# Two Newton steps, folded constants, a copy on Pool and wider w_down rows in a decode kernel

## The chip, the cores and the metric

The kernel runs on one core of a Trainium2 chip. The metric is device time in microseconds (us) of one execution, smaller is better. A core has five engines with queues of their own: PE (matrix products; its weight loads are listed as PEld), DVE and ACT (elementwise work and reductions), Pool (elementwise work, no access to the accumulators), and SP, which here only issues transfers. Work on one engine runs in program order; between engines only semaphores order it.

## The reference, cut to what matters

Two layers of a decoder for one new token of four sequences (B = 4, D = 512). In each layer an attention block with a cache of 4096 positions (32 query heads on 8 key/value heads of width 128) and a gated block (F = 1792):

```python
def _layernorm(x, eps=1e-5):
    m = jnp.mean(x, axis=-1, keepdims=True); v = jnp.var(x, axis=-1, keepdims=True)
    return (x - m) / jnp.sqrt(v + eps)

def _A_ref(x, k_cache, v_cache, wq, wo):          # attention with cached k, v
    q = (x @ wq).reshape(B, Sq, Hq, Dh)...
    p = _softmax(jnp.einsum("bhqd,bhkd->bhqk", q, k) * Dh ** -0.5)
    return einsum("bhqk,bhkd->bhqd", p, v)... @ wo

def _B_ref(x, w_gate, w_up, w_down):
    h = _sigmoid(x @ w_gate) * (x @ w_up)
    return h @ w_down

x = x + _A_ref(_layernorm(x), ...); x = x + _B_ref(_layernorm(x), ...)   # layer 1
x = x + _A_ref(_layernorm(x), ...); x = x + _B_ref(_layernorm(x), ...)   # layer 2, same weights and caches
```

## The kernel before

The caches are 64 blocks of 1 MB (K and V, for 4 sequences and 8 heads); together with the weights some 123 MB come in. Twelve slots of 1 MB hold blocks. Layer 2 reads the same caches, and part of them (K of heads 4 to 7, V of heads 6 and 7) is kept from layer 1 where the order allows; the rest is loaded again. `ORDER` writes out by hand in which order the 64 pairs of layer, sequence and head are worked on, two heads at a step; `loads` is the matching list of transfers, and `pump` issues the next ones on SP as soon as a slot is free. The eight parts of w_o and the parts of w_gate, w_up and w_down are spread between the first blocks of the caches (`wparts`).

One step of the main loop takes two heads through: `k_turn` (L872) transposes a K block in place on DVE in 32 x 32 squares; `q_blocks` (L646) lays the query out on Pool; `scores` (L889) multiplies on PE; `smax` (L904), `spread_max` (L909) and `softmax` (L919, L927) find the maximum and take exp; `ptrans` (L943, L975) turns the probabilities, with 16 small copies on ACT; `pv` (L991) multiplies with V of the step before, and `do_wo` (L1048, L1062) with w_o, adding into the residual `xT`.

When one sequence is through its attention in layer 1, its way to layer 2 is a *pass*: `pass_steps(b)` lists twelve parts, which PLACE2 and PLACE3 put into the gaps of the next two steps:

- `ln_a` (L479 to L504) sums x over partitions with a matmul by ones, centres it (`xc_sb`), copies that to bf16 (`xc_bf`, L499, on ACT) and squares it. `ln_b` (L556 to L544) sums the squares, and finds 1/sqrt(v + eps) by a first guess in integer arithmetic (L573) and three Newton steps: `newton_one` for one sequence, two instructions a step (L513, L521), `newton_many` for four, three a step (L533, L538, L544). The result `rs` isn't multiplied into x; it is applied to the products later. The Newton steps are written without their factors 1/2, so `rs` is off by a constant, which `RS` mends.
- `gate_row`, `up_row` (L707, L734): the products with w_gate and w_up as rows, x as weights of one column, four strips of the PE at once; tanh on ACT (L722) with the scale `rsg` (L717), and on DVE (t + 1) times up (L744). `h_turn` (L755) turns the row back to columns with four matmuls, `down` (L817) multiplies with w_down, and L827 and L837 scale and add to x.
- `ln_a`, `ln_b` again for the next layer, `q_row` twice (L772), `q_turn` (L800), `q_spread` (L620), which writes `qs` through ACT (L631).

The first norm and query, and the last norm and gated block, are done for all four sequences at once (`q_mm`, `gate_up` L660 with w_gate and w_up as weights, L1234 for w_down), the last after all attention. `_Sched` only records which instruction reads and writes which named buffer and puts semaphore waits before the instruction; the order on an engine is the order of the calls.

## Time and profile before

| | |
|---|---|
| time, median of 3 runs | 329.44 us (329.06 to 331.96) |
| the profiled execution | 330.95 us, its span 329.0 us |
| PE matmul busy | 229.4 us (70%) |
| DVE busy | 189.9 us (58%) |
| ACT busy | 144.8 us (44%) |
| Pool busy | 26.6 us (8%) |
| loaded | 122.95 MB, 374 GB/s over the span |

The span is the time from the first to the last instruction in the trace; the time of the execution has some 2 us around it. A row of the page's slices splits the span in 40 parts of 8.2 us and gives tenths of busy time, PEclk the clock granted to PE in tenths, GB/s what the transfers moved. In the timeline a row has start, duration, engine, line of the kernel, operation, what is written and read, how many, and in brackets how long the engine was idle before and what released it. In the view by windows a row has the stretch, its length, the busy time (and count) of PE, PEld, DVE, ACT and Pool, the granted clock, the share of the transfer engines and GB/s. The chain of waits is followed back from the last instruction, at each step to what released it.

### The profile page before, as it was taken

Reading aid. Unit: us, or ns where it says so; the run is one execution under the profiler, and the core shown is the slowest. Engines: PE = TensorE matmul, PEld = TensorE weight load, DVE = VectorE, ACT = ScalarE, POOL = GpSimd, SP = SyncE. Lnnn points to the kernel's source line nnn. Section 1 sums busy time; section 2 is a strip of 40 time slices with the busy share of each in tenths; the row PEclk is TensorE's granted clock in tenths of the full one; section 3 lists DMA queues with packets and bytes.
Section 4 is the critical chain, followed back from the end, with each engine's and each line's share of the span. In section 5 each row is a group of like instructions: output and inputs, shape, how many; then the busy total and the mean of one; then the engine's idle time right before and its main releaser. Section 6 shows DMA issues by size and latency. Waiting matters only on the chain.

```text
span 329.0 us, 10566 instructions
## 1 busy us (share of the span) xinstructions
PE 229.4 (70%) x4412; PEld 157.4 (48%) x4412; DVE 189.9 (58%) x446; ACT 144.8 (44%) x599; POOL 26.6 (8%) x133
## 2 busy tenths in 40 slices
PE   1335614232298986869899686889878688988976
PEld 1313412221255654645656464565456456555865
DVE  6377343432474439966644896664984666429543
ACT  2005412212045177644537664453765455267620
POOL 0001000000000011000001100000110000011000
PEclk9999999999997655555775555577555557555555
DMA  7999999999999999999999999999999999999600
GB/s 277 427 422 410 400 404 401 402 375 397 404 421 416 388 342 422 419 422 415 420 360 380 417 426 416 418 408 362 368 421 426 417 415 397 383 343 423 250 2 4
DMA packets 22838, 123.63 MB, mean 376 GB/s; under 512 B 2052, under 2 KB 7944, under 8 KB 8968
## 3 DMA queue, kind: packets, MB, share of 16 engines
q1 hardware_dynamic: 22792, 122.96, 93.2%
q8 instruction: 35, 0.57, 0.7%
q14 instruction: 11, 0.09, 0.1%
HBM read 122.95 MB, written 0.00 MB: 374 GB/s over the span
## 4 chain that ended last, share of the span: by engine, by line
PE 41%; DMA 32%; SPq 15%; DVE 7%; issue 3%; POOL 1%; ACT 1%; DVEq 0%; POOLq 0%; ACTq 0%
DMA slot<-in_A_v_cache_dram 28%; PE O_ps L991 12%; SPq L349 8%; PE S_ps L889 7%; SPq L363 6%; DVE slot L872 4%; PE M_ps L772 4%; DMA slot<-in_A_k_cache_dram 3%; PE MS L909 3%; PE O_ps L1048 2%; PE M_ps L817 2%; PE M_ps L707 2%; PE MS L950 2%; DVE small L904 1%; PE M_ps L479 1%
## 5 line engine op out<-in xcount | busy, mean ns | idle before, releaser
L872 DVE STREAM_TRANSPOSE slot<-slot 128x2048 f32<-128x2048 f32 (+1 forms) x62 | 112.5, 1814 | 41.1 <-DMA slot<-in_A_k_cache_dram 41.1
L975 ACT ACTIVATE pT<-PT 32x64 bf16<-32x64 f32 x504 | 108.4, 215 | 61.8 <-PE PT L943 50.1
L991 PE MATMUL O_ps<-pT,slot 128*128 128x4 bf16 x2048 | 62.3, 166 | 34.2 <-DMA slot<-in_A_v_cache_dram 32.6
L991 PEld LDWEIGHTS O_ps<-pT,slot 128*128 128x128 bf16 x2048 | 63.1, 105 | 40.2 <-DMA slot<-in_A_v_cache_dram 33.3
L889 PE MATMUL S_ps<-slot,qz 128*16 128x512 bf16 x512 | 60.3, 620 | 5.3 <-POOL qz L646 4.7
L646 POOL COPY qz<-qs 32x32 bf16<-32x32 bf16 x128 | 26.1, 204 | 277.1 <-PE S_ps L889 142.7
L927 ACT ACTIVATE pe<-S_ps,small 128x512 bf16<-128x512 f32 x32 | 22.0, 686 | 51.7 <-issue 45.9
L909 PE MATMUL MS<-valid_f,small 128*128 128x64 f32 x64 | 21.5, 438 | 32.6 <-DVE small L904 32.6
L909 PEld LDWEIGHTS MS<-valid_f,small 128*128 128x128 f32 x64 | 15.6, 304 | 50.2 <-DVE small L904 43.5
L904 DVE TENSOR_REDUCE small<-S_ps 128x1 f32<-128x512 f32 x32 | 21.3, 666 | 16.0 <-PE S_ps L889 16.0
L1048 PEld LDWEIGHTS O_ps<-oT,wo 128*128 128x128 bf16 x640 | 19.4, 105 | 12.7 <-issue 11.9
L889 PEld LDWEIGHTS S_ps<-slot,qz 128*16 128x16 bf16 x512 | 12.4, 109 | 25.0 <-issue 18.4
L1048 PE MATMUL O_ps<-oT,wo 128*128 128x2 bf16 (+1 forms) x640 | 20.3, 166 | 0.6 <-DVE oT L1029 0.6
L1029 DVE TENSOR_TENSOR oT<-O_ps,small 128x8 bf16<-128x8 f32 (+1 forms) x33 | 5.5, 167 | 20.9 <-PE O_ps L991 20.9
L950 PE MATMUL MS<-small 128*128 128x8 f32 x64 | 17.5, 347 | 0.0
L950 PEld LDWEIGHTS MS<-small 128*128 128x128 f32 x64 | 15.9, 306 | 0.0
L958 DVE RECIPROCAL small<-MS 128x8 f32<-128x8 f32 x32 | 6.6, 207 | 15.5 <-PE MS L950 15.1
L919 DVE CUSTOM_DVE_ANT_0 MS<-MS,small 128x64 f32<-128x64 f32 x32 | 8.8, 276 | 8.5 <-PE MS L909 8.5
L772 PE MATMUL M_ps<-wq,small 128*1 128x512 bf16 x128 | 13.2, 556 | 0.0
L631 ACT ACTIVATE qs<-M_ps 128x128 bf16<-128x128 f32 x8 | 1.9, 280 | 24.7 <-PE M_ps L620 24.7
L943 PE MATMUL PT<-ident_bf,pe 128*128 128x64 bf16 x128 | 11.8, 230 | 1.3 <-ACT pe L927 1.3
L479 PE MATMUL M_ps<-small 128*128 128x4 f32 (+1 forms) x20 | 5.9, 369 | 5.5 <-DVE small L837 2.1
(86 smaller groups left out, 147.3 us busy)
## 6 DMA issues: line engine op xcount, KB each, us to landing
slot<-in_A_v_cache_dram SPq DMA_DIRECT2D x56, 1024.0 KB, 12.8
slot<-in_A_k_cache_dram SPq DMA_DIRECT2D x48, 1024.0 KB, 12.0
wq<-in_A_wq_dram SPq DMA_DIRECT2D x4, 1024.0 KB, 7.9
wo<-in_A_wo_dram SPq DMA_DIRECT2D x8, 512.0 KB, 16.1
wg<-in_B_w_gate_dram SPq DMA_DIRECT2D x4, 448.0 KB, 13.7
wu<-in_B_w_up_dram SPq DMA_DIRECT2D x4, 448.0 KB, 14.3
wd<-in_B_w_down_dram SPq DMA_DIRECT2D x2, 896.0 KB, 16.5
out_dram<-slot SPq DMA_DIRECT2D x4, 1.0 KB
```

What stands on the lines that cost most here:

```text
L349: S.dma("sp", (lambda dst, src: lambda e: e.dma_start(dst, src))(dst, src), f"wo{n}" if kind == "wo" else kind, writes=[f"{kind}{n}"])
L646: (lambda a, ps: lambda e: e.tensor_copy(qz_sb[ps, :, :, a, :], qs_sb[b][ps, :, u * REP:(u + 2) * REP].rearrange("p t (u r) -> p u t r", r ...
L772: (lambda k, st: lambda e: e.matmul(M_ps[h][32 * st:32 * st + 1, :], lhsT=xc_bf[:, k, 0:1], rhs=wv[:, k, h, :, st, :], start=(k == 0), sto ...
L872: dve(lambda e: e.transpose(kf, kf), writes=[f"s{st}"])
L889: (lambda t, b2, e_, c, r0, ul: lambda e: e.matmul(S_ps[p][r0:r0 + 4 * REP, :], lhsT=qz_sb[:, ul, t, :, :].rearrange("p a r -> p (a r)"), ...
L904: dve(lambda e: e.tensor_reduce(rm_sb, S_ps[p][:, :], AX.X, ALU.max), reads=[f"S{p}"], writes=["rm"])
L909: lambda e: e.matmul(MS[:, 0:16 * REP], lhsT=rm_sb.broadcast_to([P, P]), rhs=valid_f[:, :], start=True, stop=True),
L927: lambda e: e.activation(pe_sb.rearrange("p j m -> p (j m)"), S_ps[p][:, :], ACTF.Exp, bias=nm_sb, scale=exp_scale, accum_out=sm_sb,),
L950: lambda e: e.matmul(MS[:, 64:64 + 2 * REP], lhsT=sm_sb.broadcast_to([P, P]), rhs=head_f, start=True, stop=True),
L975: (lambda dst, frm: lambda e: e.activation(dst, frm, ACTF.Copy))(dst, frm),
L991: (lambda x, c, j: lambda e: e.matmul(O_ps[p][:, ul * REP:(ul + 1) * REP], lhsT=vv[:, x * JG + c * 4 + j, :], rhs=pT_sb[:, x, j, 2 * ul + ...
L1048: (lambda c, r: lambda e: e.matmul(O_ps[p][:, 64 + 2 * c:64 + 2 * c + nb], lhsT=wo_sb[:, us[0] * REP + r, c * P:(c + 1) * P], rhs=oT_sb[:, ...
```

## The change

- Newton has two steps rather than three, with another first guess and other constants (`RSQRT_MAGIC`, `NEWTON_1`, `NEWTON_2`).
- The constant that mends `rs` (`RS`, and 0.5 RS ahead of the gated block) is multiplied into the bf16 copy of centred x (`mult`) rather than into later results. So `rsg` (L717) and the scaling of `eye4` (L1200) go, L827 and L837 become one instruction, and some instructions lose a factor.
- The bf16 copy of a single sequence (8 of them) is done on Pool; that of four sequences stays on ACT, with a scale. A key `pf` orders it against the query blocks on Pool.
- w_down is loaded with two neighbouring rows of the matrix side by side in a partition, 2 KB at a time, the first part 8 blocks of rows and the second 6 (before: 7 and 7, rows of 1 KB). For that the order of h changes: w_gate and w_up are read in blocks of 256 columns by the rows, and with every second column as weights in `gate_up`; `h_turn` takes every second column too.

The diff, without the dropped buffers and the renamed arguments of the calls:

```diff
-    RSQRT_MAGIC = float(0x5F375A86)
+    RSQRT_MAGIC = float(0x5F1FFFF9)
+    NEWTON_1 = 2.38924456
+    NEWTON_C = 0.703952253
+    NEWTON_2 = 3.0 / NEWTON_C ** 2
-    RS = -1.0 / 8192.0
+    RS = 0.5 * NEWTON_C ** 3 * (1.0 + 3.1e-7)
...
-        "wd": lambda n: (wd_sb[:, n * KH:(n + 1) * KH, :],
-                         B_w_down[n * KH * P:(n + 1) * KH * P, :].rearrange("(k p) n -> p k n", p=P)),
+        "wd": lambda n: (wd_sb[:, 8 * n:min(8 * n + 8, KF), :].rearrange("p (k e) n -> p k e n", e=2),
+                         B_w_down[8 * n * P:min(8 * n + 8, KF) * P, :].rearrange("(k p e) n -> p k e n", p=P, e=2)),
...
-    def ln_a(b0, nb):
+    def ln_a(b0, nb, mult):
...
-        act(
-            lambda e: e.activation(xc_bf[:, :, 0:nb], xc_sb[:, :, 0:nb], ACTF.Copy),
-            reads=["rc"],
-            writes=["xcb"],
-        )
+        if nb == 1:
+            S.inst(
+                "pool",
+                lambda e: e.tensor_scalar(xc_bf[:, :, 0:nb], xc_sb[:, :, 0:nb], mult, None, op0=ALU.mult),
+                reads=["rc"] + QZ,
+                writes=["xcb", "pf"],
+            )
+        else:
+            act(
+                lambda e: e.activation(xc_bf[:, :, 0:nb], xc_sb[:, :, 0:nb], ACTF.Copy, scale=mult),
...
-        for it, three in enumerate((3.0, 12.0, 768.0)):
+        for it, three in enumerate((NEWTON_1, NEWTON_2)):
...
-                reads=[f"qs{b}"],
+                reads=[f"qs{b}", "pf"],
...
-                        lhsT=wsb[:, k, fc * P:(fc + 1) * P],
+                        lhsT=wsb[:, k, bass.ds(fc // 2 * 2 * P + fc % 2, P, step=2)],
...
-        wv = wg_sb.rearrange("p k (f d) -> p k f d", d=P)
+        wv = wg_sb.rearrange("p k (f d) -> p k f d", d=2 * P)
...
-                nt = (KF - st + 3) // 4
+                nt = (KW - st + 3) // 4
...
-                        M_ps[0][32 * st:32 * st + 1, 0:nt * P],
+                        M_ps[0][32 * st:32 * st + 1, 0:nt * 2 * P],
...
-        dve(
-            lambda e: e.tensor_scalar(rsg[:, :], rs[:, 0:1], 0.5 * RS, None, op0=ALU.mult),
...
-            lambda e: e.activation(t_row[:, :], M_ps[0][:, :], ACTF.Tanh, scale=rsg[:, 0:1]),
+            lambda e: e.activation(t_row[:, :], M_ps[0][:, :], ACTF.Tanh, scale=rs[:, 0:1]),
...
-                    M_ps[0][:, 4 * j:4 * j + 4], lhsT=row_sb[:, 0, j * P:(j + 1) * P], rhs=strips, start=True, stop=True
+                        M_ps[0][:, bass.ds(8 * t + e_, 4, step=2)],
+                        lhsT=row_sb[:, 0, bass.ds(2 * P * t + e_, P, step=2)],
+                        rhs=strips,
...
-            lambda e: e.tensor_tensor(
-                dn_sb[:, :, 0:nb],
-                M_ps[0][:, 128:128 + KD * nb].rearrange("p (k b) -> p k b", k=KD),
-                bc(rs[:, 0:nb], KD, nb),
-                ALU.mult,
-            ),
...
-                out=xT[:, :, bsl(b0, nb)], in0=dn_sb[:, :, 0:nb], scalar=0.5 * RS, in1=xT[:, :, bsl(b0, nb)],
+                out=xT[:, :, b0], in0=M_ps[0][:, 128:128 + KD], scalar=rs[:, 0:1], in1=xT[:, :, b0],
                 op0=ALU.mult, op1=ALU.add,
...
-            lambda: ln_a(b0, 1),
+            lambda: ln_a(b0, 1, 0.5 * RS),
...
-    dve(lambda e: e.tensor_scalar(eye4, eye4, 0.5 * RS, None, op0=ALU.mult), writes=["eye4"])
```

More of the change, by code (lines that the diff above doesn't have):

```diff
@@ L225, in bass_interleave_layers__gqa_block_cached__glu_gated_glu__decode_kernel @@
     rowk_f = small(1)
-    rsg = small(1)
     rm_sb = small(1)
@@ L237, in bass_interleave_layers__gqa_block_cached__glu_gated_glu__decode_kernel @@
     nt_b = small(Bn)
-    nt_c = small(Bn)
     lnsum, lnsq = nt_a, nt_b
@@ L497, in ln_a @@
         )
-        act(
-            lambda e: e.activation(xc_bf[:, :, 0:nb], xc_sb[:, :, 0:nb], ACTF.Copy),
-            reads=["rc"],
-            writes=["xcb"],
-        )
+        if nb == 1:
[8 more added lines that the diff above has]
+                lambda e: e.activation(xc_bf[:, :, 0:nb], xc_sb[:, :, 0:nb], ACTF.Copy, scale=mult),
+                reads=["rc"],
+                writes=["xcb"],
+            )
         dve(
@@ L530, in newton_many @@
         y, yk = y0, "y0i"
-        for it, three in enumerate((3.0, 12.0, 768.0)):
+        for it, three in enumerate((NEWTON_1, NEWTON_2)):
             dve(
@@ L600, in q_mm @@
             dve(
[L601 to L607 removed]
+                lambda e: e.tensor_tensor(
+                    qT_sb[:, 0:HQ * nb].rearrange("p (h b) -> p h b", h=HQ),
+                    M_ps[0][:, 0:HQ * nb].rearrange("p (h b) -> p h b", h=HQ),
+                    bc(rs[:, 0:nb], HQ, nb),
+                    ALU.mult,
                 ),
@@ L752, in h_turn @@
         fns = []
-        for j in range(4):
-            fns.append(
-                (lambda j: lambda e: e.matmul(
-                    M_ps[0][:, 4 * j:4 * j + 4], lhsT=row_sb[:, 0, j * P:(j + 1) * P], rhs=strips, start=True, stop=True
-                ))(j)
-            )
+        for t in range(2):
+            for e_ in range(2):
+                fns.append(
+                    (lambda t, e_: lambda e: e.matmul(
+                        M_ps[0][:, bass.ds(8 * t + e_, 4, step=2)],
+                        lhsT=row_sb[:, 0, bass.ds(2 * P * t + e_, P, step=2)],
+                        rhs=strips,
+                        start=True,
+                        stop=True,
+                    ))(t, e_)
+                )
         S.group("pe", fns, reads=["ra"] + IDENT, writes=["M0"])
@@ L805, in q_turn @@
         dve(
-            lambda e: e.tensor_scalar(qT_sb[:, 0:HQ], M_ps[0][:, 0:HQ], RS, None, op0=ALU.mult),
+            lambda e: e.tensor_copy(qT_sb[:, 0:HQ], M_ps[0][:, 0:HQ]),
             reads=["M0"],
```

42 lines of the change are left out of this document (14 added, 28 removed).

## The prediction

> **What bounds the kernel now.** I read the page first: span, slices, chain of waits.
>
> ```profile
> span 329.0 us, 10566 instructions
> PEclk9999999999997655555775555577555557555555
> DMA  7999999999999999999999999999999999999600
> GB/s 277 427 422 410 400 404 401 402 375 397 404 421 416 388 342 422 419 422 415 420 360 380 417 426 416 418 408 362 368 421 426 417 415 397 383 343 423 250 2 4
> PE 41%; DMA 32%; SPq 15%; DVE 7%; issue 3%; POOL 1%; ACT 1%; DVEq 0%; POOLq 0%; ACTq 0%
> ```
>
> The transfer engines are busy in nearly every slice, so this is a streaming kernel, but the rate is not level: it dips in slices 14, 20 and 21, 27 and 28, 33 to 35 (slices of 8.2 us). Those are the four passes, in which one batch row's second half of a layer and the next query are squeezed between attention steps. The last three slices move almost nothing. The view by windows gives the level and the dips:
>
> ```profile
> 69.00:76.00 7.00, 4.39 (x86) 2.86 (x86) 2.45 (x3) 2.97 (x14) 0.82 (x4) 1.00 1.09 356
> 128.00:144.00 16.00, 12.73 (x226) 8.16 (x226) 14.43 (x21) 11.79 (x52) 2.45 (x12) 0.50 1.01 421
> 172.00:176.00 4.00, 3.26 (x51) 1.75 (x52) 1.13 (x4) 3.27 (x16) 1.46 (x8) 0.50 0.91 291
> 276.00:294.00 18.00, 15.86 (x276) 9.56 (x274) 6.15 (x26) 9.40 (x38) 1.64 (x8) 0.52 0.97 365
> ```
>
> The last column is GB/s. Undisturbed streaming is 421; behind a pass it falls to 291. The chain in order of time shows why: it alternates between PE work of a pass and one long transfer after it.
>
> ```profile
> 133.78 14.60 DMA slot<-in_A_v_cache_dram
> ...
> 250.04 13.76 DMA slot<-in_A_v_cache_dram
> ```
>
> A transfer starts when PE has finished with a slot. A pass that makes PE late frees slots late, the queue runs thin, and the bytes come later. After the later one lands, at 263.8, the chain is PE and DVE to the end. So time saved on the path of a pass shows at the end; time saved beside it doesn't.
>
> **The pass, and what two Newton steps are worth.** The timeline of pass 1, first half (all engines, selected rows; the last bracket is idle time of that engine before the row):
>
> ```profile
> 151.99 0.17 DVE L491 SCALAR_TENSOR_TENSOR t_row<-small 128x4 f32<-128x4 f32 x1
> 153.60 0.22 ACT L499 ACTIVATE small<-t_row 128x4 bf16<-128x4 f32 x1
> 154.01 1.87 PE L707 MATMUL M_ps<-wg,small 128*1 128x512 bf16 x16
> 155.81 0.69 PE L909 MATMUL MS<-valid_f,small 128*128 128x64 f32 x2
> 156.08 0.22 DVE L513 SCALAR_TENSOR_TENSOR small<-small 128x1 f32<-128x1 f32 x1
> 156.53 0.22 DVE L513 SCALAR_TENSOR_TENSOR small<-small 128x1 f32<-128x1 f32 x1
> 156.78 0.16 DVE L521 SCALAR_TENSOR_TENSOR small<-small 128x1 f32<-128x1 f32 x1
> 156.97 0.15 DVE L717 TENSOR_SCALAR small<-small 128x1 f32<-128x1 f32 x1
> 157.09 0.29 DVE L919 CUSTOM_DVE_ANT_0 MS<-MS,small 128x64 f32<-128x64 f32 x1
> 157.31 2.31 DVE L872 STREAM_TRANSPOSE slot<-slot 128x2048 f32<-128x2048 f32 x1
> 159.54 0.65 DVE L744 SCALAR_TENSOR_TENSOR t_row<-t_row,M_ps 128x512 bf16<-128x512 f32 x1
> 160.28 0.24 PE L755 MATMUL M_ps<-ident_bf,t_row 128*128 128x4 bf16 x4 [0.77 <-issue]
> 162.64 0.17 DVE L827 TENSOR_TENSOR t_row<-M_ps,small 128x4 f32<-128x4 f32 x1 [1.34 <-PE M_ps L817]
> 162.84 0.17 DVE L837 SCALAR_TENSOR_TENSOR small<-t_row,small 128x4 f32<-128x4 f32 x1
> 163.06 0.59 PE L479 MATMUL M_ps<-small 128*128 128x4 f32 x2 [0.53 <-DVE small L837]
> 167.61 0.43 PE L909 MATMUL MS<-valid_f,small 128*128 128x64 f32 x2
> 168.19 0.29 DVE L919 CUSTOM_DVE_ANT_0 MS<-MS,small 128x64 f32<-128x64 f32 x1 [0.19 <-PE MS L909]
> ```
>
> PE waits 0.77 us at L755 (the turn of the h row) although the page calls the releaser "issue": it needs L744, which ends at 160.19 and stands behind an unbroken DVE queue, Newton, L717, L919, one K transpose. One Newton step is two instructions, start to start 156.53 - 156.08 = 0.45 us; without the step and without L717 the last Newton instruction would end at 156.94 - 0.45 = 156.49. L919 can't start at once: it needs the PE product of L909, which ends at 156.50, and the last two rows show what a release by L909 takes: end 168.04, start 168.19, so 0.15 us. So it starts at about 156.65 instead of 157.09, and all behind it is 0.44 us earlier: the wait of 0.77 becomes 0.33. The rest of Newton's gain is eaten by L909, which is late next.
>
> Then the residual add. L827 and L837 run 162.64 to 163.01, and PE's L479 waits 0.53 us for them. They become one instruction with a per-partition scalar; L513, of that kind, takes 0.22. I take 162.64 to 162.86, so 0.15 us less, in each of the four passes.
>
> The other passes, and the second half:
>
> ```profile
> 100.96 0.96 PE L991 MATMUL O_ps<-pT,slot 128*128 128x4 bf16 x32 [0.68 <-DMA slot<-in_A_v_cache_dram]
> 218.11 0.25 PE L755 MATMUL M_ps<-ident_bf,t_row 128*128 128x4 bf16 x4 [0.68 <-issue]
> 275.70 0.24 PE L755 MATMUL M_ps<-ident_bf,t_row 128*128 128x4 bf16 x4 [0.46 <-issue]
> 172.86 1.89 PE L889 MATMUL S_ps<-slot,qz 128*16 128x512 bf16 x16 [0.74 <-POOL qz L646]
> 225.90 1.03 PE L772 MATMUL M_ps<-wq,small 128*1 128x512 bf16 x16
> 283.73 1.88 PE L772 MATMUL M_ps<-wq,small 128*1 128x512 bf16 x16
> ```
>
> Passes 2 and 3 have 0.68 and 0.46 us of the same wait, so 0.44 fits in both. Pass 0 has none there: the matmul group ahead of L755 waits 0.68 us for a V transfer, which covers it. In the second half of each pass the shorter Newton chain is worth nothing: PE runs its queue through q, softmax and PV, and its one wait (0.74 at L889) is for the Pool copies of the query blocks, which the edit leaves alone. Sum over the passes: 3 x (0.44 + 0.15) + 0.15 = 1.92 us.
>
> **The copy on Pool.** It moves 8 copies of 0.22 us from ACT, where each stood behind 16 copies of P, to Pool. The input is there at 152.16 (end of L491), PE wants the result at 154.01, so a Pool copy of up to 1.85 us costs nothing; that cover is PE's score matmuls, and if it were gone every us over it would delay L707. The nearest Pool row:
>
> ```profile
> L646 POOL COPY qz<-qs x128: 200/204/210, 22.0 to 304.0; 32x32 bf16<-32x32 bf16 x128
> ```
>
> 0.20 us for 32 elements per partition; four f32 elements with a multiply I put at 0.2 to 0.6. Behind it on Pool stand the next query blocks, which wait for the score matmuls anyway (the L646 before L889 is the same queue). Cost zero, from both sides: the ACT copy didn't end late for PE either.
>
> **w_down with rows of 2 KB.** Half the rows for the same 1.84 MB. In 69 to 76 us, with w_down and w_o (both 1 KB rows) in flight, the rate is 356; with 8 KB rows alone 421. 1.84 MB take 5.15 us at the one and 4.36 at the other: at most 0.79 us, at least nothing. If the loss goes with the number of rows per byte, 1 KB has 7/8 and 2 KB 3/8 of it, so 4/7 goes: 0.45 us. These bytes go ahead of the V transfer that PE waits 0.68 us for at 100.96, so the 0.45 arrives.
>
> **The tail.** Here Newton is cut by three DVE instructions, and I still count nothing:
>
> ```profile
> 320.84 2.97 PE M_ps L660 x112
> 323.08 0.16 DVE L544 SCALAR_TENSOR_TENSOR small<-small 128x4 f32<-128x4 f32 x1
> 323.91 0.21 DVE L686 SCALAR_TENSOR_TENSOR t_row<-t_row,M_ps 128x56 bf16<-128x56 f32 x1 [0.15 <-PE M_ps L660]
> 55.13 0.40 PE MS L950 x2
> ```
>
> L544 is Newton's last; L686 waits for PE's gate and up products (L660), not for it. The removed scaling of eye4 runs while DVE waits for PE. What does change on the path is L660: its 112 weight loads now take every second column. They go at 2.97 / 112 = 26.5 ns each now. Below: a moving operand with a step of two (L889, the K tile) takes 1.89 us for 16 of 512 columns, and the contiguous L772 1.88, both in slices with clock 5, so a step of two costs nothing there. Above: the slowest 128-wide weights in the trace, f32 in L950, take 0.20 us a piece, 112 x 0.17 = 19.4 us more. The moving row is the nearer one (same type, same step, same memory), so I take zero.
>
> Two pages speak against this. The Trainium skill, TensorE: Matmul & The Clock Gate, section Weight-path perf modes, says the fast weight load reads 32 bits at a time, two bf16 weights; the same table allows a strided pattern. At a step of two every 32-bit read would hold one wanted weight, which is the rival of half speed below. The Trainium skill, SBUF — State Buffer, section Door 1: The DMA port swizzle (its note on cachelines), says any non-contiguous PSUM access slows matmuls, and the h turn now writes every second column. No row shows such a write; there are 16 of them at 0.06 us each (0.24 for the 4 of L755), so doubling them would add 0.24 us a pass.
>
> **Sum.** 1.92 + 0.45 = 2.4 us off the profiled 330.95 (span 329.0 and 1.95 around it), so 328.6 there. That execution was 1.5 above the median 329.44 (329.06 to 331.96), so against the median: 327.0, 0.7% faster. A measurement here tells about 1% (3.3 us) from no change, so the forecast is "within 1%".
>
> **Rivals.**
> Strided weights are slow (the other side). If a step of two takes the load off its fast way, L660 grows on the path with nothing over it. It decides from 21 ns a load, where 112 x 21 = 2.4 us eats the gain; from 51 ns it is over 1% slower. At half the f32 price, 100 ns, for half the bytes: 112 x 73.5 = 8.2 us, and the 4 x 4 loads of the h turn 1.2 more: 336.4. For it: nothing in the trace has 128 weights at a step. Against: L889. Chance 0.10.
>
> Strided weights at half speed. Each of the 112 loads takes 26.5 ns more, 3.0 us, and the 16 of the h turn 0.4: 330.4, no change. This is what the Trainium skill's 32-bit rule, above, would give. For and against it, the same rows. Chance 0.08.
>
> The passes are hidden behind the transfers. If landing times are set by bytes alone, passes 0 to 2 give nothing back and only pass 3 (0.59) and the rows (0.45) count: 328.4. For it: 14 us of transfer stand behind each pass in the chain. Against: the rate drops to 291 behind a pass, so the queue does run dry. Chance 0.18.
>
> The clock joins in. L772 took 1.03 us at 225.90, in a slice whose granted clock is 7 tenths on the page, and 1.88 at 283.73, in one with 5. So pass 3 got no faster stretch in its second half. A shift of the schedule may give it one (0.85 us, and with L909, 0.43 against 0.69 in the rows above, 1.1) or take one from another pass. If it gives one, 325.9, over 1% faster. Chance 0.25; losing one (328.1) lies within the forecast.
>
> Pool is slow, so the copy doesn't do what it should: at 3 us it delays L707 1.2 us, eight times, 9.6 us: 336.6. Against it stands the 0.20 of L646. Chance 0.02.
>
> The forecast itself, 326.2 to 328.3: 0.37. The range for 8 in 10 reaches past the clock's gain (325.0) and past the half speed case by what the h turn's writes may add (331.0). Faster by over 1%: the clock's case and the low edge, 0.27; slower by over 1%: strided loads at 100 ns, Pool, and 0.01 for both mild costs together, 0.13; within 1%: 0.60.
>
> **What would show it.** Right: L755's wait in passes 1 to 3 down to 0.2 to 0.35 us, none in pass 0; L479's from 0.53 to about 0.38; L919 waiting for PE L909 instead of following Newton; the Pool copy done before L707 starts and ACT's L499 kept only for the two four-row norms; the rate at 69 to 76 above 356; L660 still 2.97. Wrong: L660 above 4 us; L707 waiting for Pool; dips behind the passes as deep as now with the chain's transfers landing at the same times.

## The result, and the profile after

| | before | after |
|---|---|---|
| time, median of 15 runs | 330.21 us (329.06 to 331.96) | 327.52 us (325.46 to 328.90) |
| ratio, after to before | | 0.9897, 95% 0.9872 to 0.9922 |
| the profiled execution, its span | 330.95, 329.0 us | 327.52, 325.6 us |
| DVE busy, instructions | 189.9 us, 446 | 184.9 us, 415 |
| ACT busy | 144.8 us | 143.1 us |
| Pool busy | 26.6 us | 28.2 us |

The kernel is 1.0% faster: 2.7 us by the medians, 3.4 us (2.6 to 4.2) by the ratio. (The 329.44 us that stands above as the median before is that of the first three of its 15 runs.) The forecast was 327.0 us and 2.4 us less than before, so the time fits and the gain was put somewhat low. The forecast time counted from the median of the first three runs; counted from that of all 15, the same 2.4 us would have given 327.8. Line numbers have moved: L707 is now L713, L734 L735, L744 L745, L755 L757, L772 L778, L817 L823, L872 L869, L889 L886, L909 L906, L919 L916, L991 L988, L646 L652, L660 L666, L686 L692; L717 is gone, and L827 and L837 are now L834.

From the page of after: the span, the granted clock, GB/s by slice, and the chain by engine.

```profile
span 325.6 us, 10554 instructions
PEclk9999999999997655555786555575555558655555
GB/s 274 433 418 407 406 404 403 400 391 406 405 421 419 401 375 412 423 418 419 423 335 419 417 424 421 417 407 400 353 422 422 417 422 418 391 370 422 254 2 5
PE 40%; DMA 33%; SPq 14%; DVE 7%; issue 2%; POOL 1%; ACT 1%; DVEq 0%; POOLq 0%; ACTq 0%
```

It is the same streaming kernel; the dips behind the passes are still there, but narrower (counted from 0, slices 20 and 21 had 360 and 380 GB/s, now 335 and 419; slices 33 to 35 had 397, 383 and 343, now 418, 391 and 370). The view by windows of after, the same four stretches as before:

```profile
69.00:76.00 7.00, 4.40 (x86) 2.86 (x86) 2.33 (x3) 3.08 (x15) 0.81 (x4) 1.00 1.06 388
128.00:144.00 16.00, 13.02 (x254) 9.04 (x246) 13.62 (x20) 10.91 (x48) 2.44 (x12) 0.50 1.01 421
172.00:176.00 4.00, 3.97 (x115) 3.51 (x103) 1.36 (x6) 2.69 (x11) 0.81 (x4) 0.59 1.01 418
276.00:294.00 18.00, 15.68 (x250) 8.27 (x242) 7.33 (x23) 9.29 (x38) 2.13 (x11) 0.59 0.99 385
```

The loading of w_down and w_o went from 356 to 388 GB/s. Undisturbed streaming is 421 as before. The third row (291 before) compares two different moments, since the schedule has moved forward by 1.4 us there (the scores that follow the pass start at 171.43 instead of 172.86), and the granted clock in it is 0.59 rather than 0.50.

The timeline of after, pass 1, first half, the rows that answer to those of before:

```profile
150.43 0.17 DVE L491 SCALAR_TENSOR_TENSOR t_row<-small 128x4 f32<-128x4 f32 x1
150.69 0.23 POOL L501 TENSOR_SCALAR small<-t_row 128x4 bf16<-128x4 f32 x1 [8.29 <-DVE t_row L491]
152.46 1.87 PE L713 MATMUL M_ps<-wg,small 128*1 128x512 bf16 x16
154.26 0.69 PE L906 MATMUL MS<-valid_f,small 128*128 128x64 f32 x2
154.53 0.22 DVE L521 SCALAR_TENSOR_TENSOR small<-small 128x1 f32<-128x1 f32 x1
154.78 0.16 DVE L529 SCALAR_TENSOR_TENSOR small<-small 128x1 f32<-128x1 f32 x1
155.10 0.29 DVE L916 CUSTOM_DVE_ANT_0 MS<-MS,small 128x64 f32<-128x64 f32 x1 [0.16 <-PE MS L906]
157.54 0.65 DVE L745 SCALAR_TENSOR_TENSOR t_row<-t_row,M_ps 128x512 bf16<-128x512 f32 x1
158.29 0.24 PE L757 MATMUL M_ps<-ident_bf,t_row 128*128 128x4 bf16 x4 [0.31 <-issue]
161.04 0.51 PE L823 MATMUL M_ps<-t_row,wd 128*128 128x1 bf16 x14 [0.89 <-issue]
161.59 0.22 DVE L834 SCALAR_TENSOR_TENSOR small<-M_ps,small 128x4 f32<-128x4 f32 x1 [2.40 <-PE M_ps L823]
161.87 0.59 PE L479 MATMUL M_ps<-small 128*128 128x4 f32 x2 [0.32 <-DVE small L834]
```

Newton's last instruction (L529) ends at 154.94, and L916, which followed Newton without a gap before, now waits 0.16 us for PE's L906. PE's wait at the turn of the h row has gone from 0.77 to 0.31 us, that for the residual add from 0.53 to 0.32. The Pool copy is done at 150.92, 1.54 us before PE starts the gate row.

The same waits in the other passes, and PE's waits for V, that is, for a block of the V cache (timeline of after, selected rows):

```profile
100.30 0.97 PE L988 MATMUL O_ps<-pT,slot 128*128 128x4 bf16 x32 [1.10 <-DMA slot<-in_A_v_cache_dram]
171.43 1.04 PE L886 MATMUL S_ps<-slot,qz 128*16 128x512 bf16 x16 [1.03 <-POOL qz L652]
204.53 1.01 PE L988 MATMUL O_ps<-pT,slot 128*128 128x4 bf16 x32 [3.02 <-DMA slot<-in_A_v_cache_dram]
215.94 0.24 PE L757 MATMUL M_ps<-ident_bf,t_row 128*128 128x4 bf16 x4
223.76 1.88 PE L778 MATMUL M_ps<-wq,small 128*1 128x512 bf16 x16
261.67 1.01 PE L988 MATMUL O_ps<-pT,slot 128*128 128x4 bf16 x32 [2.99 <-DMA slot<-in_A_v_cache_dram]
269.08 1.03 PE L735 MATMUL M_ps<-wu,small 128*1 128x512 bf16 x16
271.60 0.96 PE L988 MATMUL O_ps<-pT,slot 128*128 128x4 bf16 x32 [0.60 <-DMA slot<-in_A_v_cache_dram]
272.89 0.25 PE L757 MATMUL M_ps<-ident_bf,t_row 128*128 128x4 bf16 x4 [0.34 <-issue]
```

Over the three later passes the waits at the turn of h were 0.77, 0.68 and 0.46 us; they are 0.31, 0 and 0.34. The four waits for the residual add went from 0.53 to 0.32 each. Together PE waits 1.26 + 0.84 = 2.1 us less.

A wait also changes when PE itself comes earlier or later. A steadier measure is how long after a V block the turn of the h row starts: PE waits about 3 us for such a block some 12 us ahead of the turn in each of passes 1 to 3, before and after. For pass 2 this is, in before,

```profile
206.25 1.01 PE L991 MATMUL O_ps<-pT,slot 128*128 128x4 bf16 x32 [3.00 <-DMA slot<-in_A_v_cache_dram]
```

The turn at 218.11 starts 11.86 us behind it; in after it is 215.94 - 204.53 = 11.41. Passes 1 to 3 have 11.85, 11.86 and 11.86 us before, 11.41, 11.41 and 11.22 after: the turn starts 0.44, 0.45 and 0.64 us sooner, where the waits say 0.46, 0.68 and 0.12.

The V block of pass 0 lands at 100.30 instead of 100.96, the one between passes 2 and 3 at 261.67 instead of 263.84: 0.66 us early becomes 2.2 us early, so the gain comes in on the way and through the transfers. It does not follow the waits stretch by stretch. From V block to V block (100.30, 146.88, 204.53, 261.67, end of the span) the stretches went from 47.47 to 46.58, from 57.82 to 57.65, from 57.59 to 57.14 and from 65.16 to 63.93 us. Pass 1, where the waits fell by 0.67, gave only 0.17; in it PE stopped for 0.89 us inside L823 (161.04 above), which it did not do there before. And the first stretch took 46.58 to 47.92 us in four traces with the same code up to there (after, and the three kernels below that are late in pass 1 or pass 3 only), so one such stretch is known to about 1 us.

In pass 3 some is given back, 0.60 us of a V wait that was not there before. In the chain of after the last transfer is the one to that block, which lands within pass 3:

```profile
256.27 15.28 DMA slot<-in_A_v_cache_dram
```

The tail (timeline of after). L666 is the former L660:

```profile
317.26 1.63 PE L666 MATMUL M_ps<-small,wg 128*128 128x4 bf16 x56
320.50 0.21 DVE L692 SCALAR_TENSOR_TENSOR t_row<-t_row,M_ps 128x56 bf16<-128x56 f32 x1 [0.74 <-PE M_ps L666]
```

In the chain of waits of after, as in that of before (2.97 us), it is one piece:

```profile
317.43 2.96 PE M_ps L666 x112
```

So the weights at a step of two cost nothing. The three DVE instructions that went from Newton only lengthen the wait of the next one, 0.15 to 0.74 us.

### The profile page after: what moved, and what is told of

Read it like the earlier page. It is cut to its first block, busy times and chain, and to the rows that moved or that the text cites. A ratio compares the mean times of both kernels' runs of the same rounds, so it can differ in the third digit from the quotient of the medians.

```text
span 325.6 us, 10554 instructions
## 1 busy us (share of the span) xinstructions
PE 227.5 (70%) x4412; PEld 156.1 (48%) x4412; DVE 184.9 (57%) x415; ACT 143.1 (44%) x591; POOL 28.2 (9%) x141
## 4 chain that ended last, share of the span: by engine, by line
PE 40%; DMA 33%; SPq 14%; DVE 7%; issue 2%; POOL 1%; ACT 1%; DVEq 0%; POOLq 0%; ACTq 0%
DMA slot<-in_A_v_cache_dram 29%; PE O_ps L988 12%; SPq L349 8%; PE S_ps L886 7%; SPq L363 6%; DVE slot L869 4%; PE M_ps L778 4%; DMA slot<-in_A_k_cache_dram 4%; PE MS L906 3%; PE O_ps L1045 2%; PE M_ps L823 2%; PE MS L947 2%; DVE small L901 2%; PE M_ps L479 1%; PE PT L940 1%
## 5 line engine op out<-in xcount | busy, mean ns | idle before, releaser
L869 DVE STREAM_TRANSPOSE slot<-slot 128x2048 f32<-128x2048 f32 (+1 forms) x62 | 112.4, 1813 | 40.8 <-DMA slot<-in_A_k_cache_dram 40.8
L988 PE MATMUL O_ps<-pT,slot 128*128 128x4 bf16 x2048 | 62.7, 166 | 34.1 <-DMA slot<-in_A_v_cache_dram 33.4
L988 PEld LDWEIGHTS O_ps<-pT,slot 128*128 128x128 bf16 x2048 | 63.3, 105 | 39.9 <-DMA slot<-in_A_v_cache_dram 34.3
L886 PE MATMUL S_ps<-slot,qz 128*16 128x512 bf16 x512 | 59.4, 612 | 5.8 <-POOL qz L652 5.2
L906 PE MATMUL MS<-valid_f,small 128*128 128x64 f32 x64 | 21.5, 438 | 32.0 <-DVE small L901 32.0
L652 POOL COPY qz<-qs 32x32 bf16<-32x32 bf16 x128 | 26.0, 203 | 192.1 <-PE S_ps L886 115.5
L906 PEld LDWEIGHTS MS<-valid_f,small 128*128 128x128 f32 x64 | 15.6, 303 | 49.1 <-DVE small L901 42.8
L886 PEld LDWEIGHTS S_ps<-slot,qz 128*16 128x16 bf16 x512 | 12.4, 109 | 25.2 <-issue 17.8
L955 DVE RECIPROCAL small<-MS 128x8 f32<-128x8 f32 x32 | 6.7, 208 | 15.1 <-PE MS L947 14.6
L916 DVE CUSTOM_DVE_ANT_0 MS<-MS,small 128x64 f32<-128x64 f32 x32 | 8.8, 276 | 10.9 <-PE MS L906 10.3
L778 PE MATMUL M_ps<-wq,small 128*1 128x512 bf16 x128 | 13.5, 568 | 0.0
```

The source lines that it names most:

```text
L652: (lambda a, ps: lambda e: e.tensor_copy(qz_sb[ps, :, :, a, :], qs_sb[b][ps, :, u * REP:(u + 2) * REP].rearrange("p t (u r) -> p u t r", r ...
L778: (lambda k, st: lambda e: e.matmul(M_ps[h][32 * st:32 * st + 1, :], lhsT=xc_bf[:, k, 0:1], rhs=wv[:, k, h, :, st, :], start=(k == 0), sto ...
L869: dve(lambda e: e.transpose(kf, kf), writes=[f"s{st}"])
L886: (lambda t, b2, e_, c, r0, ul: lambda e: e.matmul(S_ps[p][r0:r0 + 4 * REP, :], lhsT=qz_sb[:, ul, t, :, :].rearrange("p a r -> p (a r)"), ...
L906: lambda e: e.matmul(MS[:, 0:16 * REP], lhsT=rm_sb.broadcast_to([P, P]), rhs=valid_f[:, :], start=True, stop=True),
L988: (lambda x, c, j: lambda e: e.matmul(O_ps[p][:, ul * REP:(ul + 1) * REP], lhsT=vv[:, x * JG + c * 4 + j, :], rhs=pT_sb[:, x, j, 2 * ul + ...
```

## The experiments

Each kernel is an edit of the kernel after, except the two that do one part alone on the kernel before. "Worth" is the difference of two ratios times 330.2 us, and such a difference is known to about 1.4 us either way (the two intervals added in squares), and to about 1.9 us for the two kernels with the widest intervals, rows of 1 KB and late second halves. The diffs show the main lines only (`...` where lines are left out); that of a delay which repeats an earlier one is against the earlier one.

### One part undone

**Three Newton steps again.**

```diff
-    RSQRT_MAGIC = float(0x5F1FFFF9)
+    RSQRT_MAGIC = float(0x5F375A86)
-        for it, three in enumerate((NEWTON_1, NEWTON_2)):
+        for it, three in enumerate((3.0, 12.0, 768.0)):
```

> The changed kernel with three Newton steps again, with the constants of before; all else as changed. Path theory (a step saves 0.45 us of DVE in the first half of a pass, which PE sees at the turn of the h row, and the transfers pass it on): PE's wait at the turn of the h row in passes 1 to 3 is 0.3 to 0.45 us longer than in the changed kernel (0.31, 0, 0.34), in sum 1 to 1.3 us, and the time is 0.3 to 0.4% above the changed kernel's, at a ratio to before of about 0.993. Rival, hidden behind transfers: only pass 3 counts, 0.4 us, a ratio of about 0.991. Tail: the products of gate and up still take 2.96 us and the instruction after them still waits for PE, so nothing there.

Measured: ratio 0.9944 (0.9915 to 0.9973). In its timeline, pass 1:

```profile
148.08 1.01 PE L989 MATMUL O_ps<-pT,slot 128*128 128x4 bf16 x32 [3.01 <-DMA slot<-in_A_v_cache_dram]
159.74 0.25 PE L758 MATMUL M_ps<-ident_bf,t_row 128*128 128x4 bf16 x4 [0.78 <-issue]
```

The wait is back, 0.78, 0.80 and 0.79 us in passes 1 to 3: 1.72 us more than after. Counted from the V block, the turn starts at 11.66 us in all three passes (159.74 - 148.08), 0.25, 0.25 and 0.44 later than after, 0.9 us in sum; a step of 0.45 costs only 0.25 there because with two steps the next DVE instruction waits for PE's L906. The time is 1.6 us (±1.3) more, which fits the 0.9 as well as the 1.7. So the third step does make PE late, by less than the waits say. By time alone the hidden-behind-transfers rival (0.991) lies just out of this kernel's own interval, but within it once the uncertainty of after is added.

**Rows of 1 KB again**, with the old order of h.

```diff
-        "wd": lambda n: (wd_sb[:, 8 * n:min(8 * n + 8, KF), :].rearrange("p (k e) n -> p k e n", e=2),
-                         B_w_down[8 * n * P:min(8 * n + 8, KF) * P, :].rearrange("(k p e) n -> p k e n", p=P, e=2)),
+        "wd": lambda n: (wd_sb[:, n * KW:(n + 1) * KW, :],
+                         B_w_down[n * KW * P:(n + 1) * KW * P, :].rearrange("(k p) n -> p k n", p=P)),
...
-                        lhsT=wsb[:, k, bass.ds(fc // 2 * 2 * P + fc % 2, P, step=2)],
+                        lhsT=wsb[:, k, fc * P:(fc + 1) * P],
```

> The changed kernel with w_down loaded in rows of 1 KB again, and with it the old order of h (no weights at a step of two). Theory: the rate at 69 to 76 us falls back from 388 to about 356 GB/s, the V block for which pass 0 waits lands 0.5 to 0.7 us later (at about 100.9 rather than 100.3), and the end is 0.45 us later: a ratio to before of about 0.991. Rival, rows carry most of the gain: 1.5 us or more, a ratio of 0.995. Rival, the strided weights cost something that other gains hid: then this kernel is faster than the changed one, with gate and up in the tail under 2.96 us.

Measured: ratio 0.9896 (0.9842 to 0.9950). The window of the weights:

```profile
69.00:76.00 7.00, 4.39 (x86) 2.86 (x86) 2.61 (x3) 2.81 (x14) 0.76 (x4) 1.00 1.10 359
```

The rate falls from 388 to 359, and the first V block lands at 101.06 instead of 100.30. The time can't tell 0.4 us, but the landing can: over eleven traces with 2 KB rows it lies between 100.25 and 100.59, over three with 1 KB rows between 100.80 and 101.06, some 0.5 us apart. L666 takes 2.96 us here too, with contiguous weights, so no cost of strided weights was hidden. The rival that the rows carry most of the gain (0.995) lies at the very edge of the interval.

**The copy on ACT again.**

```diff
-        if nb == 1:
+        if nb == 0:
```

> The changed kernel with the bf16 copy of one sequence on ACT again, with its scale. Theory: no difference, a ratio to before of 0.990, since the first product of a half pass starts right behind PE's own sum of squares in both. Rival, the copy on Pool is what makes the change good: PE waits before the gate row or the q row by 0.2 us or more, eight times, 1.6 us, a ratio of 0.994.

Measured: ratio 0.9914 (0.9883 to 0.9945), span 325.0 us. Timeline, pass 1:

```profile
152.39 0.59 PE L564 MATMUL M_ps<-t_row,small 128*128 128x4 f32 x2
152.50 0.21 ACT L507 ACTIVATE small<-t_row 128x4 bf16<-128x4 f32 x1
152.91 1.87 PE L713 MATMUL M_ps<-wg,small 128*1 128x512 bf16 x16
```

ACT starts the copy 1.62 us after L491, Pool did 0.26 after it, and PE still starts the gate row right behind the statistics (L564) without a wait: the copy is done at 152.71, 0.20 us before it is needed. The move to Pool is worth nothing that shows.

**The constant not folded:** the residual add in two instructions and one scaling of `rs` more, as before, with two Newton steps.

```diff
+        dve(lambda e: e.tensor_scalar(rsg[:, :], rs[:, 0:1], 1.0, None, op0=ALU.mult), ...)
...
+            lambda e: e.tensor_tensor(sq_sb[:, :, 0:nb], M_ps[0][:, 128:128 + KD * nb]..., bc(rs[:, 0:nb], KD, nb), ALU.mult),
...
-                out=xT[:, :, b0], in0=M_ps[0][:, 128:128 + KD], scalar=rs[:, 0:1], in1=xT[:, :, b0],
+                out=xT[:, :, bsl(b0, nb)], in0=sq_sb[:, :, 0:nb], scalar=1.0, in1=xT[:, :, bsl(b0, nb)],
```

> The changed kernel with the residual add of a pass as two instructions and with one extra DVE instruction ahead of tanh (a multiplication of the row's scale by 1), as the kernel before had. Theory: PE's wait for the residual add goes from 0.32 to 0.53 us in all four passes (0.8 us in sum), and the wait at the turn of the h row grows by up to 0.2 us in passes 1 to 3: 0.8 to 1.2 us, a ratio to before of about 0.993. Rival, hidden: 0.3 us, a ratio of 0.991.

Measured: ratio 0.9973 (0.9941 to 1.0006). Timeline, pass 2:

```profile
206.16 1.01 PE L1004 MATMUL O_ps<-pT,slot 128*128 128x4 bf16 x32 [3.02 <-DMA slot<-in_A_v_cache_dram]
217.57 0.25 PE L763 MATMUL M_ps<-ident_bf,t_row 128*128 128x4 bf16 x4 [0.52 <-issue]
220.81 0.59 PE L480 MATMUL M_ps<-small 128*128 128x4 f32 x2 [0.88 <-DVE small L850]
```

The folding is worth 2.5 us (±1.4), at least twice what was expected. The waits grew by 1.6: those for the residual add are 0.53, 0.53, 0.88 and 0.53 instead of four times 0.32 (1.19 more), those at the turn of h 0.56, 0.52 and 0 instead of 0.31, 0 and 0.34 (0.43 more). Not all of this is lateness by the two instructions. The turn starts 11.40, 11.41 and 11.54 us after its V block (217.57 - 206.16 in pass 2), in after 11.41, 11.41 and 11.22: in passes 1 and 2 no later, PE only came there sooner. And of the 0.88 us in pass 2, 0.45 pass between PE's last recorded product (219.93) and DVE's start (220.38), where before has 0.11; the two instructions take 0.17 us each as elsewhere. So the rows carry the 0.8 us expected of the residual add, and nothing of the scaling of `rs`; the other 1.7 (±1.4) have no row that ties them to the folding.

### One part alone, on the kernel before

**Two Newton steps alone.**

```diff
-    RS = -1.0 / 8192.0
+    RS = 0.5 * NEWTON_C ** 3 * (1.0 + 3.1e-7)
...
-        for it, three in enumerate((3.0, 12.0, 768.0)):
+        for it, three in enumerate((NEWTON_1, NEWTON_2)):
```

> The kernel before with two Newton steps and the new constants alone. Path theory: PE's wait at the turn of the h row in passes 1 to 3 is 0.3 to 0.45 us shorter (0.77, 0.68, 0.46 before), 1.2 us in sum; a ratio to before of 0.996. Rival, the fold and not Newton is what PE saw: 0.999 to 1.000.

Measured: ratio 0.9997 (0.9964 to 1.0030), span 327.8 us. In its timeline the wait at the turn of h falls to 0.18 us in pass 1 and to nothing in passes 2 and 3, while the residual add still costs 0.53, and 0.88 in pass 2:

```profile
147.32 1.02 PE L994 MATMUL O_ps<-pT,slot 128*128 128x4 bf16 x32 [2.42 <-DMA slot<-in_A_v_cache_dram]
158.74 0.24 PE L758 MATMUL M_ps<-ident_bf,t_row 128*128 128x4 bf16 x4 [0.18 <-issue]
214.91 1.01 PE L994 MATMUL O_ps<-pT,slot 128*128 128x4 bf16 x32 [1.43 <-DMA slot<-in_A_v_cache_dram]
219.02 0.59 PE L482 MATMUL M_ps<-small 128*128 128x4 f32 x2 [0.88 <-DVE small L840]
274.26 0.25 PE L758 MATMUL M_ps<-ident_bf,t_row 128*128 128x4 bf16 x4
```

The turn starts 11.42 us after its V block in pass 1 (158.74 - 147.32) and 11.41 in pass 3, instead of 11.86, so there the step does what it should. In pass 2 PE waits 1.43 us for another V block just ahead of the turn (214.91), which then starts at 11.83, as before. The span of the profiled execution is 1.2 us shorter, but 1.1 of that is there before pass 1 begins, and over twelve runs the time is the same to 0.1 us by the ratio (0.9 less by the medians, 330.34 and 331.23), with up to 1.2 us of gain left in the interval. The expected 0.996 lies just outside. Undone (above) it was worth 1.6 us ± 1.3, alone 0.1 ± 1.1: both allow 0.3 to 1.2 us, and no more can be said.

**The rows alone.**

```diff
-        "wd": lambda n: (wd_sb[:, n * KH:(n + 1) * KH, :],
+        "wd": lambda n: (wd_sb[:, 8 * n:min(8 * n + 8, KF), :].rearrange("p (k e) n -> p k e n", e=2),
...
```

> The kernel before with w_down in rows of 2 KB alone, and with it the new order of h. Theory: 69 to 76 us run at 384 to 388 rather than 356 GB/s, the V block of pass 0 lands at 100.3 to 100.5 rather than 101.0, gate and up in the tail stay at 2.97 us, and the end is 0.45 us earlier, a ratio to before of 0.9985. Rival, what is won at 100 us is lost at the next wait (PE has the pass's own work to do by then): 1.000.

Measured: ratio 0.9977 (0.9942 to 1.0013), and

```profile
69.00:76.00 7.00, 4.40 (x86) 2.86 (x86) 2.62 (x3) 2.81 (x14) 0.77 (x4) 1.00 1.06 389
```

with the V block landing at 100.59, and the tail group at 2.96 us with strided weights. Its waits at the turn are 0.18, 0.18 and 0.98 us with Newton as long as before, but the turn starts at 11.86, 11.85 and 11.86 after its V block, as before: here it is PE that comes at other times. The three parts, 0.0% (Newton alone), 0.2% (rows alone) and 0.8% (folding, undone), add to the 1.0% of the whole, each with some 0.4% of doubt. With such doubts, and with 0.5% for Newton undone, the sum is no proof of the shares.

### Is the path real? Delays put in

The strongest rival was that the passes are hidden behind the transfers. Here Newton's first product is computed again and again, with the same result each time, so that DVE is late by a chosen amount.

**About 2 us in pass 1, first half** (8 repeats).

```diff
+            for _ in range(8 if it == 0 and call == 2 else 0):
+                dve((lambda y: lambda e: e.scalar_tensor_tensor(
+                        out=nt_a[:, 0:1], in0=y, scalar=vpe[:, 0:1], in1=y, op0=ALU.mult, op1=ALU.mult))(y), ...)
```

> The changed kernel with a delay in the first half of pass 1 only: the product of the first Newton step is made eight times more with the same result, some 2.0 us of DVE. Path theory: PE's wait at the turn of the h row in pass 1 goes from 0.31 to about 2.2 us, slots come free as much later, the transfers pass it on to the end: 1.5 to 2 us over the changed kernel, a ratio to before of about 0.996. Rival, pass 1 is hidden behind the transfers that follow it: PE's wait grows as much, but the V blocks after it land at the same times, and the end moves by less than 0.5 us, a ratio of 0.990 to 0.991.

Measured: ratio 0.9928 (0.9894 to 0.9963): 1.0 us (±1.4) more than after, between the two theories. PE's wait rose from 0.31 to 1.73. The time alone can't tell them apart, the delay being small against the scatter. The trace speaks for the path: the turn starts 13.26 us after its V block instead of 11.41, and the V block ahead of pass 2 lands 59.47 us after the one ahead of pass 1 (147.33 and 206.80) instead of 57.65, so 1.8 of the 1.85 us are still there (one such stretch is known to about 1 us).

**About 5 us at the same place** (20 repeats).

```diff
-            for _ in range(8 if it == 0 and call == 2 else 0):
+            for _ in range(20 if it == 0 and call == 2 else 0):
```

> The changed kernel with the product of the first Newton step made twenty times more in the first half of pass 1 only, some 5.0 us of DVE; a dose large against the scatter of the runs. Path theory: PE's wait at the turn of the h row in pass 1 is 4.5 to 5 us, the next V block that PE waits for lands 4 us or more later, and the end is 4 to 4.7 us later: a ratio to before of about 1.003. Rival, hidden behind transfers: the V block lands at most 1 us later, a ratio of 0.990 to 0.993.

Measured: ratio 1.0037 (1.0002 to 1.0071), 4.6 us more than after. Timeline:

```profile
147.19 1.02 PE L1000 MATMUL O_ps<-pT,slot 128*128 128x4 bf16 x32 [2.68 <-DMA slot<-in_A_v_cache_dram]
163.49 0.25 PE L769 MATMUL M_ps<-ident_bf,t_row 128*128 128x4 bf16 x4 [4.62 <-issue]
209.60 1.01 PE L1000 MATMUL O_ps<-pT,slot 128*128 128x4 bf16 x32 [3.65 <-DMA slot<-in_A_v_cache_dram]
```

PE waits 4.3 us more in pass 1, its turn starts 16.30 us after its V block, 4.9 us later than after, and the V block 46 us behind the turn lands at 209.60 instead of 204.53. The transfer queue did not make up for it: the next bytes came about as late as PE. For pass 1 the rival of hidden passes (0.990 to 0.993) falls. A delay shows that lateness reaches the end; that time saved reaches it too doesn't follow from it, since a saving may end at the next V block (pass 2 of Newton alone, pass 3 of after).

**The same in pass 3**, behind which no transfer stands in the chain of before.

```diff
-            for _ in range(20 if it == 0 and call == 2 else 0):
+            for _ in range(20 if it == 0 and call == 6 else 0):
```

> The same delay of some 5.0 us in pass 3 only, behind which the chain of before has no transfer. Both theories: 4 to 4.7 us, a ratio to before of about 1.003. Told apart by the difference to the same delay in pass 1: none by the path theory, 3 to 4 us by the rival.

Measured: ratio 1.0088 (1.0055 to 1.0121), 6.3 us (±1.4) more than after.

```profile
263.89 1.01 PE L1000 MATMUL O_ps<-pT,slot 128*128 128x4 bf16 x32 [3.33 <-DMA slot<-in_A_v_cache_dram]
280.19 0.25 PE L769 MATMUL M_ps<-ident_bf,t_row 128*128 128x4 bf16 x4 [4.27 <-issue]
```

The wait grew by 3.9 us, the turn starts 16.30 us after its V block instead of 11.22, 5.1 us later, and from that V block to the end of the span the trace is 4.7 us longer than after's. The V block itself landed 2.2 us later than in after, although the code ahead of it is the same. So pass 3 costs about what the delay makes it late; the 1.2 us between 5.1 and 6.3 lie within the uncertainty, and so, nearly, does the difference to pass 1 (1.7 ± 1.6).

**About 2 us in the first half of all four passes.**

```diff
-            for _ in range(8 if it == 0 and call == 2 else 0):
+            for _ in range(8 if it == 0 and call % 2 == 0 else 0):
```

> The same delay of some 2.0 us in the first half of all four passes. Path theory: about 1.9 us in each of passes 1 to 3 and somewhat less in pass 0, where a V block covers 1 us: 6 to 7.5 us over the changed kernel, a ratio to before of about 1.010. Rival, hidden: only pass 3, 2 us, a ratio of 0.996.

Measured: ratio 1.0064 (1.0032 to 1.0097), 5.5 us more than after, where the hidden passes would have given 2. The path again, a little under the 6 to 7.5 that it foretold, which the uncertainty reaches.

**About 1.25 us in the second half of all four passes** (5 repeats), what the removed step and more would have given there.

```diff
-            for _ in range(8 if it == 0 and call == 2 else 0):
+            for _ in range(5 if it == 0 and call % 2 == 1 else 0):
```

> A delay in the second half of all four passes (five more of the same product, some 1.25 us of DVE). Theory: PE has q, softmax and PV to do there and doesn't see it: within 0.5 us of the changed kernel, a ratio to before of 0.990. Rival, the second Newton chain is on the path too: 1.25 us in each pass, 5 us, a ratio of 1.005.

Measured: ratio 0.9896 (0.9845 to 0.9946), the same as after to 1.9 us. PE waits for the query row's turn 0.18 us in pass 2 and, longest, in pass 3:

```profile
284.02 0.36 PE L818 MATMUL M_ps<-ident_bf,t_row 128*128 128x4 bf16 x8 [0.39 <-issue]
```

So Newton in the second halves is beside the path, as the prediction had it: the 5 us of the rival are ruled out, half a microsecond isn't.

The delays and the parts, by four measures: PE's waits at the turn and the residual add, the start of the turn after its V block (summed over passes 1 to 3), the trace from the V block ahead of the first pass concerned (pass 1, in the last delay pass 3) to the end of the span, and the time of the runs. The first five rows are differences to after, the last to before.

| | wait of PE, us | start of the turn, us | trace to its end, us | time, us (±1.4) |
|---|---|---|---|---|
| three Newton steps | +1.7 | +0.9 | +1.8 | +1.6 |
| not folded | +1.6 | +0.3 (and 0.8 at the add) | +2.0 | +2.5 |
| late in pass 1, 8 repeats | +1.4 | +1.9 | +1.9 | +1.0 |
| late in pass 1, 20 repeats | +4.3 | +5.0 | +4.2 | +4.6 |
| late in pass 3, 20 repeats | +3.9 | +5.1 | +4.7 | +6.3 |
| two Newton steps alone | -1.4 | -0.9 | -0.1 | -0.1 |

The large delays come out at the end about whole. For effects of 1 to 2 us the measures differ by as much as they are uncertain, and Newton alone shows that not every microsecond saved at the turn reaches the end.

### A further cut: the wait for the query blocks

After a pass PE waits for Pool's copies of the query blocks (1.03 us in pass 1 of after). Here every second copy goes to DVE.

```diff
-                "pool",
+                "dve" if late and a % 2 else "pool",
```

> The changed kernel with the four query blocks that follow a pass shared, two on Pool and two on DVE, which stands idle there. Path theory: PE's wait for them at the end of a pass goes from 0.73 to 1.03 us down to 0.3 to 0.55, in four passes 1.5 to 2 us, and the time falls by as much: a ratio to before of about 0.984. Rival, hidden: only pass 3, 0.5 us, a ratio of 0.988; or the copies on DVE hold up the softmax behind them, and nothing is won.

Measured: ratio 0.9884 (0.9846 to 0.9922), median 327.13 us. Timeline, passes 1 and 2:

```profile
171.88 0.37 DVE L652 COPY qz<-qs 32x32 bf16<-32x32 bf16 x2 [0.40 <-ACT qs L637]
172.51 1.88 PE L886 MATMUL S_ps<-slot,qz 128*16 128x512 bf16 x16 [0.30 <-POOL qz L652]
229.30 1.88 PE L886 MATMUL S_ps<-slot,qz 128*16 128x512 bf16 x16 [0.59 <-DVE small L955]
```

The wait is 0.30 us in passes 0, 1 and 3 instead of 1.02 to 1.03, and 0.59 in pass 2 instead of 0.73, where PE now waits for another DVE instruction (L955): 2.3 us of waits less in all. The end is 0.4 us earlier (±1.5), which can't be told from none, and lies at least 0.4 us short of the 2.3. So a wait taken away at this place does not seem to be worth its whole length; whether the rest is given back to the transfers, to the clock (the up row of pass 1 took 1.76 us in this trace, 1.40 in after) or to the stall told below is not settled.

## Why the prediction was right, point by point

**The turn of the h row.** Forecast: all behind Newton 0.44 us earlier in passes 1 to 3, waits left of 0.2 to 0.35, then L909 is late. Found: the turn starts 0.44, 0.45 and 0.64 us sooner after its V block. The DVE instruction that followed Newton waits 0.16 us for PE's L906 in passes 1 and 2, as foreseen (0.15); in pass 3 it doesn't wait, because L906 took 0.43 us there instead of 0.69. The waits fell by 0.46, 0.68 and 0.12, in sum 1.26 for 1.32; that this sum comes so near is partly luck, since single waits also change with PE's own arrival.

**The residual add.** Forecast 0.15 a pass, found 0.21 (0.53 to 0.32). L834 takes 0.22 us instead of the 0.37 in which two instructions ran, as foreseen. The other 0.06 lie ahead of them: in pass 1 DVE started 0.11 us after PE's wait began before (162.53 and 162.64), 0.04 after (161.55 and 161.59).

**The rows.** Forecast 0.45 us at the first V block; it came 0.66 early in this pair of traces and about 0.5 over all of them. The rate in the stretch rose to 388.

**Nothing for the Pool copy, the second halves and the tail.** All three held, as far as the runs can tell: the Pool copy took 0.23 us, inside the estimate of 0.2 to 0.6; late second halves cost nothing that shows (±1.9); the tail lost DVE work into a longer wait.

**The strided weights.** The 112 loads took 2.96 us with a step of two and 2.96 to 2.97 without, 26 ns each, so both rivals on them fall. The Trainium skill, TensorE: Matmul & The Clock Gate, section Weight-path perf modes, has the fast load read 32 bits at a time; it did not cost a load at a step of two anything here, and the same table's "packed or strided" agrees. The strided PSUM writes of the turn of h took 0.24 to 0.25 us for four (L757), 0.24 to 0.25 before (L755): the statement in the Trainium skill, SBUF — State Buffer, section Door 1: The DMA port swizzle, that any non-contiguous PSUM access slows matmuls, does not show for four columns at a step of two, which is a small test.

**Hidden passes.** The delays decide against this rival, above all the one of 5 us in pass 1; for passes 0 and 2 there is only the delay in all four (5.5 us, where it gives 2). That a saving passes on is shown by the landing times of before and after, and with Newton alone it did not in pass 2.

**The clock.** It moved, in both directions. L778 took 1.88 us at 223.76, where it had taken 1.03; in pass 3 L735 took 1.03 at 269.08, where L734 had taken 1.70:

```profile
271.85 1.70 PE L734 MATMUL M_ps<-wu,small 128*1 128x512 bf16 x16
```

That row is of before. With the other rows of pass 3 that gained 1.3 us (gate 0.34, L909 0.26, up 0.67), and 0.60 of it went into the new V wait. Pass 2 lost about as much in its second half.

**The size.** The terms as the traces give them are 1.5 us for the turn (1.26 by the waits), 0.84 for the residual add and 0.5 to 0.66 for the rows, 2.6 to 3.0 us, against 2.4 forecast. The measured gain is 3.4 (2.6 to 4.2) by the ratio and 2.7 by the medians, so the forecast gain lies just below the interval and the traced one within it. How it divides between Newton and the folding the runs do not settle. Forecast were 0.60 us for the residual add and 1.32 for Newton together with L717; measured were 2.5 ± 1.4 for the folding undone, and for Newton 1.6 ± 1.3 undone and 0.1 ± 1.1 alone. The traces put the folding at 0.84 and nothing for L717 once Newton has two steps. Whether the remainder is scatter, the clock, or something of the folding that no wait shows is open.

## What to carry to other kernels

A shortened chain is worth what it saves up to the next operand that comes late: look for that operand's row first, as L909 was here, and then at when the engine that frees the buffers gets there, counted from the last transfer that it waited for; its waits alone mislead, since they also grow when it comes sooner. Lateness there came back through the transfers nearly whole, 46 us later (4.9 us, and 4.2 to 4.6 at the end); a saving below 1 us could be lost at the next block that landed. Rows of a load can be made wider by permuting the order of a hidden dimension, if the weights that follow may be read at a step without cost, as they could here. Where runs scatter by 1%, a delay some times larger than the scatter, put at the disputed place, settles in one kernel what removing a small cost can't, though only for lateness.

## What the hardware showed that was not expected

From about 100 us on, the granted clock of a PE that is busy most of the time lies at about half (5 in most slices of the clock row, 9 in the first twelve), with short faster stretches: the same 16 matmuls of L778 take 1.03 or 1.88 us. These stretches fall at other places before and after and move a pass by about 1 us either way, as much as a term of the sum. That is one reason why single spans here do not decide between small theories.

PE also stops inside a group of matmuls whose operands have all been there: 0.89 us within the 56 products of w_down (L823) in pass 1 of after, in the timeline above, and at the same place, after 42 of the 56, in the kernel with shared query blocks:

```profile
162.32 0.51 PE L823 MATMUL M_ps<-t_row,wd 128*128 128x1 bf16 x14 [1.20 <-issue]
```

Nothing in the trace releases it. Six of the 14 traces have it, 0.30 to 1.20 us long, always in pass 1 and in no other pass; before doesn't. It was not tested what it is.

The residual add's wait was 0.88 us instead of 0.53 in pass 2 in both kernels that had two instructions there with two Newton steps (above, not folded, and Newton alone). The added 0.35 us lie between PE's last recorded product and the start of the first of the two; why is open.
